# Windowed attention and a gated network on one Trainium2 core: weights by 1024 columns, values in one load, first keys copied, second unit's steps by twos

## The chip, the cores and the metric

The kernel runs on one core of a Trainium2 chip. The metric is the device time of one execution in microseconds (us), lower being better. The core has five engines that take their instructions in order and wait for each other by semaphores: TensorE (PE in the profile; PEld is its loading of weights), VectorE (DVE), ScalarE (ACT), GpSimd (POOL) and SyncE (SP), which here issues nearly all loads.

## The reference

```
attention: q, k, v are (4, 8, 768, 64)
k_sum = max of k over blocks of 32 rows;  v_sum = mean of v over blocks of 32 rows
scores_l = scale * q k^T, masked to |i - j| < 16
scores_s = scale * q k_sum^T + log(32)
a = softmax of the two side by side;  out = a @ [v; v_sum]
network: x is (3072, 512), the attention's output by tokens
h = ((x @ w1) * (x @ w2)) @ w3          w1, w2: (512, 1024), w3: (1024, 1024)
return h @ w_out                        w_out: (1024, 512)
```

The network's weights are 64-bit floats; q, k, v are 32-bit.

## The kernel before

**Network.** `w3 @ w_out` is folded once into eight tiles `wp` (`fold_weights`, L192). Then, for each unit of 512 tokens (six units), `gate` (L413) makes eight hidden tiles `h` out of w1 and w2, and `project` (L445) multiplies them by `wp`. Every product is split in a high and a low part and costs three matmuls with 512 columns (`products`, L110): 192 matmuls for the fold, and 192 for the gates and 96 for the projections of one unit.

**Weights.** A weight arrives as pairs of 32-bit words. `weight` and `start_loads` (L127, L135) load it in pieces of 512 columns (512 KB) into a ring of ten tiles, on SP. `convert` (L151) makes floats of it: a Prelu on ScalarE for every piece (L166), on VectorE a shift (L174) and for every piece a shift-and-or (L177), then the high part by a cast on ScalarE (L187) and the low part by a subtraction on VectorE (L108, in the helper `low`). Most weights have 1024 columns in two pieces; wo 0 and w3 0 to 3 are handled by halves.

**Attention.** A step is one unit with one of four pairs of heads, 24 steps. `load_scores` (L297) loads q and k, k in four windows of 160 columns with a gap of 24 into which `gather` (L305) copies the block summaries on GpSimd; `load_values` (L277) loads the values in three DMAs and `load_sums` (L286) adds the value means. Then: scores on TensorE (L320), masking and maximum on VectorE (L334), exponential on ScalarE (L348), reciprocal (L353, L354), normalization, transposes on TensorE (L374), copies `pt` out of PSUM (L379 to L383), outputs on TensorE (L394) and x (L405, L108). The summaries of batch 0 come from whole keys (`load_keys`, L222; `summaries`, L227) and from value rows whose block means TensorE makes (`mean_products`, L256); those of batch 1 are loaded as eight `raw` tiles through two buffers (`load_second`, `second_batch`).

**Order.** The first two units (steps 0 to 7) run in a loop whose counter `t` counts weight pieces. `LOADS` (L598) tells which input is loaded after which piece, `WORK` (L614) what else is done at which `t`, `FIRST` at which `t` a step begins: its scores are issued there, and at the next step's `t` its transposes and copies, its outputs one `t` later. After this, `run` (L499) issues so many columns of the network's products to TensorE, as far as their weights are there: `RATE` a step of the loop, `LATER_RATE`, and at last an even share of what is left up to the end of the first unit. In this loop SP and TensorE keep the program's order; the other engines' order is made by the planner. After it, the steps 8 to 23 run by twos in slots, with two steps' scores beside the transposes and outputs of the two before, and a stretch of the network behind them. `NORMALIZE` tells for each of the steps 0 to 7 whether ScalarE (A, eight instructions, L363) or VectorE (V, one, L365) normalizes, `SECOND` who makes the second copy `pt`.

Of the kernel before, what the change touches and what calls it, by code (L numbers as in the profile page):

```python
# [11 lines left out]
F32 = mybir.dt.float32  # L12
# [15 lines left out]
PIECE = 512  # L28
AHEAD = 4

FIRST = (15, 18, 20, 22, 27, 32, 37, 44)
# [3 lines left out]
EARLY = (  # L35
    *(("wo", 0, 0), ("w3", 0, 0), ("wo", 0, 1), ("w3", 1, 0), ("wo", 1), ("w3", 2, 0), ("w3", 3, 0)),
    *(("w3", 0, 1), ("w3", 1, 1), ("wo", 2), ("w3", 2, 1), ("w3", 3, 1), ("wo", 3)),
)
# [9 lines left out]
NORMALIZE = "VAAAAAAA"  # L48
SECOND = "AAAVAVVA"
SOONER = 400  # L50
RING = 10
# [19 lines left out]
def attention_moe(ctx, tc, qG, kW, kT, vP, vW, vB, mask, w1, w2, w3T, wo, out):  # L71
    nc = tc.nc
    B, NPAIR, _, S = kT.shape
    NB = S // BLOCK
# [20 lines left out]
    ident = const.tile([P, P], F32, name="ident")  # L95
    make_identity(nc, ident)
    mask_sb = const.tile([P, 3, KR], F32, name="mask_sb")

    mean_sb = const.tile([P, S // P * NB], F32, name="mean_sb")
    nc.gpsimd.memset(mean_sb, 0.0)  # L100
    for i in range(P // BLOCK):
        part = mean_sb[i * BLOCK : (i + 1) * BLOCK, i : S // P * NB : NB + P // BLOCK]
        nc.gpsimd.memset(part, 1.0 / BLOCK)
# [23 lines left out]
    def weight(name, i, src, shape, part=None):  # L127

        n = src.shape[1] // 2
        parts = range(n // PIECE) if part is None else [part]  # L130
        units.append((name, i, shape, list(parts), len(todo) + len(parts) - 1))
        for k in parts:
            todo.append(src[:, 2 * k * PIECE : 2 * (k + 1) * PIECE])

    def start_loads(at_least):  # L135

        while todo or due_loads:
            if len(loading) >= at_least and len(loading) + len(working) + len(kraws) + len(vraws) + made[0] + 2 >= RING:
                return
# [8 lines left out]
            due_loads.extend(LOADS.pop(begun[0], ()))  # L148
            begun[0] += 1

    def convert(name, i, shape, parts, last):  # L151


        n = len(parts) * PIECE
        f = sb.tile([P, 2 * PIECE], F32, name="wf", bufs=5)[:, :n]
        bits = f.bitcast(U32)
        low_words = []
# [3 lines left out]
        for k in range(len(parts)):  # L161
            raw = loading.pop(0)
            working.append(raw)
            words = raw.rearrange("p (n t) -> p n t", t=2)
            low_words.append(words[:, :, 0])
            nc.scalar.activation(  # L166
                f[:, k * PIECE : (k + 1) * PIECE],
# [51 lines left out]
    def held(b):  # L219
        return {"bufs": 2} if b else {"tag": "ring", "bufs": RING}  # L220

# [555 lines left out]
```

## Time and profile before

| | |
|---|---|
| timed runs | 538.26, 538.26, 539.84 us (median 538.26) |
| profiled execution | 540.01 us, span 537.9 us |
| busy share of the span | PE 96%, PEld 78%, ACT 45%, DVE 44%, POOL 11% |
| granted TensorE clock, mean | 0.994 |
| moved by DMA | 67.21 MB |

The span goes from the first to the last instruction. A line such as L320 is a line of the program below. In the lists, a group gives line, engine, operation, written and read tiles and their shapes, the count, the busy time in us, the mean of one in ns, and then the idle time of the engine before it and what ended it ("<-"). In the chain of waits each row is start, length and what the end of the program waited for at that time.

### The profile page before, as it was taken

To read this page: it belongs to the slowest core of one execution; us is meant where nothing else is said; L and a number is where in the kernel's file an instruction comes from. 1 tells how busy PE (TensorE), PEld (TensorE's weight loads), DVE (VectorE), ACT (ScalarE), POOL (GpSimd) and SP (SyncE) were. 2 spreads that over 40 slices of the span, in tenths; PEclk is the share of its full clock that TensorE was granted. 3 is DMA by queue.
4 is the path that set the end of the run, shared out by engine and by line. 5 is a ranking of instruction groups with operands and counts; after the bars stand their busy time and mean duration, and the time that the engine had idled before them with its cause. 6 is when DMAs were issued, how large, how long until landed. Compare 5 with 4: busy or idle time off the path is not lost.

```text
span 537.9 us, 9987 instructions
## 1 busy us (share of the span) xinstructions
PE 514.2 (96%) x3888; PEld 419.8 (78%) x3888; DVE 237.2 (44%) x686; ACT 239.7 (45%) x691; POOL 56.8 (11%) x99
## 2 busy tenths in 40 slices
PE   2877999999999999999999999999999999999997
PEld 1655777778778888888888888888888888888885
DVE  4878989998404236634244033251042250122210
ACT  5548998886436226226245144262162361222210
POOL 0020121111002101103003003011011030000000
PEclk9988999999999999999999999999999999999999
DMA  8999899595524005544041141050160021000001
GB/s 300 399 347 346 219 293 372 172 295 172 177 76 153 0 1 169 160 125 142 0 125 45 40 151 60 0 165 25 40 190 1 1 75 39 22 19 0 1 19 58
DMA packets 30574, 67.21 MB, mean 125 GB/s; under 512 B 4032, under 2 KB 7616, under 8 KB 30528
## 3 DMA queue, kind: packets, MB, share of 16 engines
q1 hardware_dynamic: 27072, 60.30, 35.5%
q10 hardware_dynamic: 3456, 6.29, 3.2%
q8 instruction: 30, 0.49, 0.4%
q14 instruction: 16, 0.13, 0.1%
HBM read 58.51 MB, written 6.29 MB: 120 GB/s over the span
## 4 chain that ended last, share of the span: by engine, by line
PE 83%; DMA 9%; ACT 5%; DVE 1%; issue 0%; SPq 0%; ACTq 0%
PE mm L112 74%; DMA wraw<-in_w3T_dram 5%; PE po L394 4%; PE sc L320 3%; DMA raw<-in_kT_dram 3%; PE tp L374 2%; DMA v<-in_vW_dram 2%; ACT sm L348 2%; ACT sm L363 1%; ACT w L187 1%; ACT wf L166 1%; ACT pt L379 0%; DVE wf L177 0%; ACT x L405 0%; ACT wp L210 0%
## 5 line engine op out<-in xcount | busy, mean ns | idle before, releaser
L112 PE MATMUL mm<-x,w 128*128 128x512 f32 x1152 | 265.2, 390 | 0.0
L112 PEld LDWEIGHTS mm<-x,w 128*128 128x128 f32 x1152 | 215.3, 188 | 46.0 <-DVE w L108 0.3
L112 PE MATMUL mm<-wp,h 128*128 128x512 f32 x576 | 134.0, 391 | 0.0
L112 PEld LDWEIGHTS mm<-wp,h 128*128 128x128 f32 x576 | 107.5, 188 | 22.8 <-issue 0.2
L348 ACT ACTIVATE sm<-sm,mx 128x120 f32<-128x120 f32 x192 | 73.6, 388 | 19.9 <-DVE mx L334 19.9
L439 DVE TENSOR_TENSOR g<-mm,g 128x512 f32<-128x512 f32 x48 | 33.1, 689 | 89.3 <-PE mm L112 87.5
L440 ACT CAST h<-g 128x512 fp32r<-128x512 f32 x48 | 29.7, 618 | 88.4 <-DVE g L439 88.4
L112 PE MATMUL mm<-w,w 128*128 128x512 f32 x192 | 53.0, 428 | 12.6 <-ACT w L187 11.4
L112 PEld LDWEIGHTS mm<-w,w 128*128 128x128 f32 x192 | 37.3, 202 | 25.0 <-ACT w L187 13.3
L458 ACT COPY o<-mm 128x512 f32<-128x512 f32 x24 | 14.0, 585 | 81.4 <-PE mm L112 81.4
L108 DVE TENSOR_TENSOR h<-g,h 128x512 fp32r<-128x512 f32 x48 | 35.9, 748 | 25.1 <-ACT h L440 24.8
L436 ACT COPY g<-mm 128x512 f32<-128x512 f32 x48 | 28.0, 583 | 34.5 <-PE mm L112 34.1
L334 DVE CUSTOM_DVE_ANT_0 sm<-sc,mask_sb 128x120 f32<-128x120 f32 x192 | 40.9, 275 | 2.9 <-PE sc L320 2.9
L383 DVE COPY pt<-tp 120x512 f32<-120x512 f32 x19 | 12.4, 687 | 67.6 <-PE tp L374 67.6
L307 POOL COPY k<-ks 128x96 f32<-128x96 f32 (+1 forms) x32 | 9.8, 316 | 257.3 <-DMA k<-in_kW_dram 194.7
L348 ACT ACTIVATION_READ_ACCUMULATOR sm<-sm,mx 128x1 f32 x192 | 36.7, 191 | 0.0
L108 DVE TENSOR_TENSOR x<-po,x 128x512 fp32r<-128x512 f32 x24 | 16.6, 691 | 42.3 <-ACT x L405 42.3
L166 ACT ACTIVATE wf<-wraw 128x512 f32<-128x512 f32 x40 | 26.4, 673 | 8.3 <-DMA wraw<-in_wo_dram 3.9
L357 POOL TENSOR_TENSOR sm<-sm,mx 128x960 f32<-128x960 f32 x16 | 29.1, 1820 | 6.0 <-DVE mx L354 5.0
L394 PEld LDWEIGHTS po<-pt,v 120*64 120x64 f32 x768 | 23.9, 138 | 5.8 <-issue 2.5
L108 DVE TENSOR_TENSOR w<-wf,w 128x1024 fp32r<-128x1024 f32 (+1 forms) x25 | 25.4, 1015 | 5.8 <-ACT w L187 5.5
L394 PE MATMUL po<-pt,v 120*64 120x64 f32 x768 | 26.3, 224 | 1.6 <-ACT pt L379 1.4
(33 smaller groups left out, 273.2 us busy)
## 6 DMA issues: line engine op xcount, KB each, us to landing
k<-in_kW_dram SPq DMA_DIRECT2D x24, 368.0 KB
wraw<-in_w3T_dram SPq DMA_DIRECT2D x16, 512.0 KB
wraw<-in_w_dram SPq DMA_DIRECT2D x16, 512.0 KB
q<-in_qG_dram SPq DMA_DIRECT2D x24, 256.0 KB
raw<-in_kT_dram SPq DMA_DIRECT2D x16, 384.0 KB
out_dram<-o ACTq DMA_DIRECT2D x24, 256.0 KB
v<-in_vW_dram SPq DMA_DIRECT2D x24, 192.0 KB
raw<-in_vB_dram SPq DMA_DIRECT2D x12, 384.0 KB
```

Source lines behind the costliest of these rows:

```text
L108: eng.tensor_tensor(dst, src, hi.bitcast(F32), ALU.subtract)
L112: nc.tensor.matmul(acc, lhsT=a, rhs=b, start=first and i == 0, stop=last and i == len(terms) - 1)
L166: nc.scalar.activation(f[:, k * PIECE : (k + 1) * PIECE], words[:, :, 1].bitcast(F32), AF.Prelu, scale=2.0**-112, alpha=-(2.0**32),)
L320: nc.tensor.matmul(sc[h][64 * g : 64 * g + 64, i * KR : (i + 1) * KR], lhsT=q[rows, i * P + 64 * g : i * P + 64 * g + 64], rhs=k[rows, i, ...
L334: nc.vector.tensor_tensor_reduce(out=sm[:, j], in0=sc[h][:, i * KR : (i + 1) * KR], in1=mask_sb[:, 0 if blk == 0 else 2 if blk == BLOCKS - ...
L348: nc.scalar.activation(sm[:, j], sm[:, j], AF.Exp, bias=mx[:, 0, j : j + 1], scale=-1.0, accum_out=mx[:, 1, j : j + 1])
L357: nc.gpsimd.tensor_tensor(sm, sm, mx[:, 2].unsqueeze(2).broadcast_to([P, NI, KR]), ALU.mult)
L394: nc.tensor.matmul(po[cols, at : at + 64], lhsT=v[:, g, i, cols], rhs=pt[g][:, (h * NBLK + i) * 64 : (h * NBLK + i + 1) * 64], start=True, ...
L436: nc.scalar.copy(g, a[:, :U])
L439: nc.vector.tensor_tensor(g, acc[1][:, :U], g, ALU.mult)
L440: nc.scalar.copy(h[:, 0], g)
L458: nc.scalar.copy(o, acc[:, :DO])
```

## The change

- `PIECE` is 1024 and the ring has five tiles of double size, with two loads ahead instead of four. A weight of 1024 columns is one load of 1 MB, and its Prelu, shift, shift-and-or, cast and subtraction are one instruction each. Only the first two weights are still converted by halves of 512. w3's first four tiles are stored so that one load holds half of two of them (`w3h`).
- Hidden tiles `h` lie in pairs in one ring tile. Whole keys and value rows of batch 0 take the buffers of x (six) instead of the ring's.
- A step's values come in one DMA, with zero rows where the means are added.
- The first unit's steps no longer load k: `windows` copies it on GpSimd out of the whole keys, in two copies a step.
- `FIRST` is now (12, 18, 20, 23, 46, 62): steps 0 to 3 begin one by one at the first four, and step 3's transposes wait for 46. Steps 4 and 5 begin together at 46; at 62 their transposes and outputs are issued and steps 6 and 7 begin. The transposes and outputs of 6 and 7 move into the first slot. Before the slots, the network is issued up to 0.96 of the first unit instead of all of it.
- `NORMALIZE`, `SECOND`, `LOADS`, `WORK` and the rates have new values; P stands for GpSimd. Steps 0 and 1 transpose into the scores' PSUM banks. The copies out of the folded products have a higher priority.

```diff
-PIECE = 512
-AHEAD = 4
-FIRST = (15, 18, 20, 22, 27, 32, 37, 44)
+PIECE = 1024
+AHEAD = 2
+FIRST = (12, 18, 20, 23, 46, 62)
-EARLY = (
-    *(("wo", 0, 0), ("w3", 0, 0), ("wo", 0, 1), ("w3", 1, 0), ("wo", 1), ("w3", 2, 0), ("w3", 3, 0)),
-    *(("w3", 0, 1), ("w3", 1, 1), ("wo", 2), ("w3", 2, 1), ("w3", 3, 1), ("wo", 3)),
-)
+EARLY = (("wo", 0), ("w3h", 0), ("wo", 1), ("w3h", 2), ("w3h", 1), ("wo", 2), ("w3h", 3), ("wo", 3))
-NORMALIZE = "VAAAAAAA"
-SECOND = "AAAVAVVA"
+NORMALIZE = "APAPPVVV"
+SECOND = "VVAVVAVV"
+BANKS = "SSTTTTST"
-RING = 10
+RING = 5
...
-            if len(loading) >= at_least and len(loading) + len(working) + len(kraws) + len(vraws) + made[0] + 2 >= RING:
+            if len(loading) >= at_least and len(loading) + len(working) + (made[0] + 1) // 2 + 1 >= RING:
...
+        n = PIECE // 2 if first < 4 else PIECE
+        parts = [slice(k, k + n) for k in range(0, PIECE, n)]
...
-        return {"bufs": 2} if b else {"tag": "ring", "bufs": RING}
+        return {"bufs": 2} if b else {"tag": "x", "bufs": 6}
...
-        nc.sync.dma_start(v[:CUT, 0], vW[u, p, 0])
-        nc.sync.dma_start(v[: CUT - 64, 1], vW[u, p, 1, : CUT - 64])
-        nc.sync.dma_start(v[KR - 64 :, 1], vW[u, p, 1, CUT - 64 :])
+        nc.sync.dma_start(v, vW[u, p])
...
-        nc.sync.dma_start(k, kW[p, :, u * NBLK : (u + 1) * NBLK])
+        if u:
+            nc.sync.dma_start(k, kW[p, :, u * NBLK : (u + 1) * NBLK])
         return q, k
+
+    def windows(k, raw):
+
+        for to, at in ((k[:, :, :CUT], 0), (k[:, :, CUT + NB :], CUT)):
+            nc.gpsimd.tensor_copy(to, raw[:, at : at + U].rearrange("p (i c) -> p i c", c=P)[:, :, : to.shape[2]])
...
+        if NORMALIZE[s] != "A":
+            eng = nc.vector if NORMALIZE[s] == "V" else nc.gpsimd
+            eng.tensor_tensor(sm, sm, mx[:, 2].unsqueeze(2).broadcast_to([P, NI, KR]), ALU.mult)
...
-        h = sb.tile([P, 2, U], F32R, name="h", tag="ring", bufs=RING)
+        if f % 2 == 0:
+            pair_of_h[0] = sb.tile([P, 2, 2, U], F32R, name="h", tag="ring", bufs=RING)
+        h = pair_of_h[0][:, f % 2]
...
+    TO_SLOTS = ALL_FOLD + 0.96 * UNIT
...
+    def two_pairs(s):
+
+        both = [begin(p) for p in (s, s + 1)]
+        yield
+        for p, (u, sm, mx, sc) in zip((s, s + 1), both):
+            reduce(u, 0, sc, sm, mx)
+            reduce(u, 1, sc, sm, mx)
+            expose(0, sm, mx)
+            yield
+            expose(1, sm, mx)
+            invert(mx)
+            yield
+            normalize_alone(p, sm, mx)
+
+    def four_pairs(s):
+
+        steps = two_pairs(s)
+        yield from steps
+        while t[0] < FIRST[-1]:
+            yield
+        steps = two_pairs(s + 2)
+        tps = [transposes(sms.pop(p)[0], **more) for p, more in zip((s, s + 1), ({}, SPARE))]
+        pts = [evacuate(tp, SECOND[p]) for p, tp in zip((s, s + 1), tps)]
+        next(steps)
+        for p, pt in zip((s, s + 1), pts):
+            keep_x(outputs(pt, values.pop(p)), xs[place(p)[0]])
+        yield
+        yield from steps
...
+    def first_keys(p):
+        raw = kraws.pop(p)
+        windows(inputs[p][1], raw)
+        summaries(0, p, raw)
...
     LOADS = {
+        4: [lambda: keys(0)],
         7: [lambda: nc.sync.dma_start(mask_sb, mask)],
+        8: [lambda: fetch(0)],
+        9: [lambda: rows(1)],
+        11: [lambda: fetch(1)],
+        15: [lambda: rows(2), lambda: rows(0)],
+        16: [lambda: keys(1), lambda: keys(2)],
+        17: [lambda: fetch_values(0), lambda: keys(3)],
+        18: [lambda: fetch(2)],
+        23: [lambda: fetch_values(1), lambda: fetch_values(2)],
+        25: [lambda: fetch(3)],
+        26: [lambda: fetch_values(3)],
     }
     WORK = {
+        11: [lambda: first_keys(0), lambda: fill(0)],
+        13: [means],
+        17: [lambda: load_second(2), lambda: fetch_sums(0)],
+        18: [lambda: first_keys(1), lambda: fill(1)],
+        20: [lambda: first_keys(2), lambda: fill(2)],
+        21: [lambda: load_second(0), lambda: load_second(1), lambda: fetch(5), lambda: fetch_sums(2)],
+        22: [lambda: second_batch(0), lambda: load_second(3), lambda: load_second(4), lambda: first_keys(3), lambda: fetch(4), lambda: fill(3), lambda: fetch_sums(1)],
+        23: [lambda: second_batch(1)],
+        24: [lambda: load_second(5)],
+        25: [lambda: second_batch(2), lambda: second_batch(4), lambda: load_second(6)],
...
+        31: [lambda: second_batch(5)],
...
+        34: [lambda: fill(4)],
...
+        40: [lambda: fill(5)],
...
     }
-    RATE = 6600
-    LATER_RATE = 6944
+    RATE = 8000
+    LATER_RATE = 2744
...
-                due = given[0] + (ALL_FOLD + UNIT - given[0]) / max(1, FIRST[-1] + 7 - t[0])
-            run(min(due, ALL_FOLD + UNIT))
+                due = given[0] + (TO_SLOTS - given[0]) / max(1, FIRST[-1] + 5 - t[0])
+            run(min(due, TO_SLOTS))
...
-            last = (s - 2, s - 1) if s > NFIRST else ()
+            last = (s - 2, s - 1)
```

216 lines of the change are left out of this document (104 added, 112 removed).

## The prediction

> **What bounds the kernel now.** I read the page's head first, then the chain of waits, then TensorE's timeline in the first 90 us, and last the groups and windows of that stretch.
>
> ```profile
> span 537.9 us, 9987 instructions
> PE 514.2 (96%) x3888; PEld 419.8 (78%) x3888; DVE 237.2 (44%) x686; ACT 239.7 (45%) x691; POOL 56.8 (11%) x99
> ```
>
> The profiled execution took 540.01 us, 2.1 us more than its span; the three timed runs have a median of 538.26 us. I work out a difference against the profiled execution and take it off the median. A difference of 0.3% (1.6 us) is about what a measurement of this kernel can tell from none.
>
> TensorE is busy 96% of the span, so only its waits can be won. The chain of waits (start, length, what) says where they lie:
>
> ```profile
> 86.19 0.04 issue
> 86.24 1.15 PE po L394 x32
> 87.39 13.84 PE mm L112 x60
> 101.23 0.61 PE tp L374 x16
> 101.84 0.98 PE sc L320 x32
> 102.83 3.67 PE mm L112 x15
> 106.49 1.08 PE po L394 x32
> ...
> 278.57 32.86 PE mm L112 x144
> ...
> 534.42 0.59 ACT o L458
> ```
>
> From 86.24 us on the chain is TensorE's almost without a break. So the end is (the moment at which the gates of the first unit begin, 87.4 us) + (TensorE's work from there on). I call that moment G. A change that doesn't alter the products moves the end one for one with G, plus any wait that it makes later. Prices of TensorE's pieces: 0.228 us a product (32.86/144), 0.61 for a step's transposes, 0.98 for its scores, 1.08 for its outputs.
>
> Before G, TensorE's own timeline and windows of the stretch show what was lost:
>
> ```profile
> 36.03 0.64 PE L261 MATMUL means<-rows,mean_sb 128*24 128x128 f32 x16 [2.63 <-DMA rows<-in_vP_dram]
> 49.82 0.69 PE L374 MATMUL tp<-ident,sm 64*120 64x64 f32 x16 [3.37 <-DVE sm L365]
> 86.24 1.15 PE L394 MATMUL po<-pt,v 120*64 120x64 f32 x32 [1.21 <-ACT pt L379]
> ```
>
> ```profile
> 0.00:87.00 87.00, 66.98 (x586) 49.81 (x588) 69.31 (x161) 63.23 (x160) 12.31 (x32) 0.96 0.97 323
> 10.00:30.00 20.00, 16.93 (x57) 11.22 (x57) 17.20 (x28) 11.90 (x19) 0.00 (x0) 1.00 1.03 400
> 36.00:40.00 4.00, 3.97 (x38) 2.79 (x42) 1.91 (x3) 2.65 (x6) 2.76 (x4) 0.62 1.04 356
> 50.00:54.00 4.00, 4.00 (x52) 3.28 (x50) 3.93 (x7) 2.69 (x4) 0.00 (x0) 0.57 1.02 332
> 60.00:80.00 20.00, 19.83 (x219) 15.44 (x219) 17.34 (x55) 20.00 (x70) 3.93 (x9) 1.00 0.86 246
> ```
>
> (Columns of the second: stretch, then busy us of PE, weight loads, DVE, ACT, POOL, then granted clock, DMA share, GB/s.) The products for the block means end at 36.67. Between them and G stand, in program order, 126 of the 192 weight-folding products, four steps' transposes, five steps' scores and four steps' outputs: 126 x 0.228 + 4 x 0.61 + 5 x 0.98 + 4 x 1.08 = 40.4 us. 36.67 + 40.4 = 77.1, and G was 87.4. So 10.3 us were lost after the means: 3.4 waiting for step 0's normalization, 1.2 for step 3's copy, 1.5 and 1.7 to a clock of 0.62 and 0.57 in the 4 us after an idle stretch, the rest in small pieces while ScalarE was busy 20.00 of 20 us.
>
> **The change part by part.**
>
> *The means.* They wait for the three loads of value rows. Ahead of the last of those in SP's order before: 16 weight pieces, mask, one q, one k, two sets of whole keys. After: 8 weight pieces of double size, mask, two q, one set of keys.
>
> ```profile
> k<-in_kW_dram SPq DMA_DIRECT2D x24, 368.0 KB
> q<-in_qG_dram SPq DMA_DIRECT2D x24, 256.0 KB
> raw<-in_kT_dram SPq DMA_DIRECT2D x16, 384.0 KB
> ```
>
> That is 368 + 384 - 256 = 496 KB less, less 8 KB for the padding: 1.2 us at the 400 GB/s of 10 to 30 us. Means end at 35.4. The first product now needs 2 MB instead of 1 MB, 2.6 us later at that rate; the idle time before the means hides it, and without that cover it costs 2.6.
>
> *TensorE's order after the means.* By the step at which each weight is ready, 20 products (60 matmuls) stand before the means instead of 66 matmuls, so 132 follow. Step 3's transposes and outputs, and the gates, are moved from loop step 27/28 to 46/47; between the end of the fold (25) and 46 nothing else is issued to TensorE, so its order keeps its form, with one exception: the scores of step 5 now stand ahead of step 3's outputs and of the gates, not only those of step 4. Work: 132 x 0.228 + 4 x 0.61 + 5 x 0.98 (scores 1 to 5) + 4 x 1.08 = 41.8 us. Floor of G: 35.4 + 41.8 = 77.2. The 0.98 of step 5 comes off the work behind G.
>
> *ScalarE and VectorE until G.* The groups:
>
> ```profile
> L166 ACT ACTIVATE wf<-wraw 128x512 f32<-128x512 f32 x40 | 26.4, 673 | 8.3 <-DMA wraw<-in_wo_dram 3.9 <-DMA wraw<-in_w3T_dram 2.3 <-DMA wraw<-in_w_dram 2.0
> L187 ACT CAST w<-wf 128x1024 fp32r<-128x1024 f32 x15 | 15.7, 1049 | 6.2 <-DVE wf L177 6.1
> L177 DVE SCALAR_TENSOR_TENSOR wf<-wraw,wf 128x512 uint32<-128x512 uint32 x40 | 26.3, 685 | 0.5
> L108 DVE TENSOR_TENSOR w<-wf,w 128x1024 fp32r<-128x1024 f32 x15 | 18.5, 1233 | 4.2 <-ACT w L187 4.2
> L363 ACT ACTIVATE sm<-sm,mx 128x120 f32<-128x120 f32 x56 | 17.9, 395 | 0.9 <-DVE mx L354 0.9
> L383 DVE COPY pt<-tp 120x512 f32<-120x512 f32 x3 | 2.1, 687 | 1.1 <-PE tp L374 1.1
> L365 DVE TENSOR_TENSOR sm<-sm,mx 128x960 f32<-128x960 f32 x1 | 1.2, 1151 | 0.0
> L357 POOL TENSOR_TENSOR sm<-sm,mx 128x960 f32<-128x960 f32 x2 | 4.0, 2018 | 0.3 <-DVE mx L354 0.3
> ```
>
> A 1024-wide Prelu doesn't occur: between 1.05 (the 1024-wide cast) and 1.35 us (two of 512); I take 1.10, since the cast does the same pass. 14 units are converted up to G, 12 of them now in one piece: 12 x (1.35 - 1.10) = 3.0 us off ScalarE. The 1024-wide L177: between 1.23 (L108 of that width) and 1.37; I take 1.23, because it too reads two SBUF operands: 12 x 0.14 = 1.7 us off VectorE. Normalization of steps 0 to 3 was V, A, A, A and is A, P, A, P: ScalarE does 16 passes of 0.395 instead of 24 (-3.2), VectorE loses 1.15, GpSimd gains two of 2.02. Second copies were A, A, A, V and are V, V, A, V: two of about 0.6 leave ScalarE, 2 x 0.69 come to VectorE. Sums until G: ScalarE 7.4 us less, VectorE -1.7 - 1.2 + 1.4 = 1.5 less. From the 0:87 row, VectorE needs some 68 of its 69.3 us; its first work can begin at about 6 us, so its floor for G is 74, below TensorE's 77.2. ScalarE's is near 62. So the next bound is TensorE itself.
>
> *Step 0 is begun earlier.* Its whole keys are the first input loaded and it begins at loop step 12 instead of 15, with more products between its scores and its transposes. The 3.4 us wait and the slow clock behind it (1.7) go. The slow clock after the means (1.5) stays. The Trainium skill ("TensorE: Matmul & The Clock Gate", the HAM clock gate) says that an idle window of about 3.4 us halves the clock until one has been busy; the two rows fit, and by that rule a shorter gap before the means would save that 1.5 too. I keep it.
>
> *Moved copies.* The first unit's k loads (4 x 368 KB, 3.8 us of DMA time) become two GpSimd copies a step. On GpSimd's queue stand behind them the filling-in of the summaries, the inversions and the value sums. Nearest rows:
>
> ```profile
> 32.20 0.58 POOL L307 COPY k<-ks 128x96 f32<-128x96 f32 x1 [30.33 <-DVE ks L229]
> 40.68 0.26 POOL L307 COPY k<-ks 128x96 f32<-128x96 f32 x1
> 75.61 0.22 POOL L307 COPY k<-ks 128x48 f32<-128x48 f32 x1
> ```
>
> (0.26 - 0.22)/48 is 0.8 ns an element, so 384 and 256 elements take about 0.5 and 0.4 us: 0.9 a step alone, twice that beside VectorE's work. Steps 0, 2 and 3 have their keys long before; step 1's lie under the products of the fold. Nothing on the path; 0.9 to 1.8 if step 1's keys come late.
>
> *One load of values a step* issues one DMA instead of three, and moves 480 KB instead of 384 (zero rows): 0.25 us a step, off the path. *Halved ring of doubled tiles, hidden layer in pairs*: same bytes, nothing.
>
> *New waits.* Step 1's normalization on GpSimd takes 2.0 instead of eight passes; I allow 1 us before its transposes. Step 5's scores need the second batch's keys for it, loaded late on SP's queue (worked out with the first rival); I allow 1.5. With the clock (1.5), 4.0 us are lost after the means instead of 10.3. G = 77.2 + 4.0 = 81.2, 6.2 earlier.
>
> *Behind G.* The second unit's steps go by twos: 4 and 5 right before G, 6 and 7 at loop step 62, with two transposes moved into the first slot of the main loop. Between the scores of 6 and 7 and their transposes lie two outputs and some 33,700 columns (66 products), 17 us; the chain of two steps on VectorE and ScalarE needs 13 to 15. I allow 1.0 us for a wait there (0 to 3). The later slots are unchanged.
>
> Sum: -6.2 (G) - 1.0 (scores of 5 already done) + 1.0 = -6.2. The profiled 540.01 becomes 533.8, the median 538.26 becomes 532.0.
>
> **The rivals.**
>
> *Slower: the scores of step 5 hold the gates.* In SP's order the keys for step 5 stand behind q 4, which waits for the scores of step 3 to free a buffer, behind values 3 and behind two-buffer loads of the second batch. All of TensorE waits in order behind scores 5. The waits exist already:
>
> ```profile
> SPq L281 <- PE po L394: 20.8, 4, 12.6
> SPq L301 <- PE sc L320: 9.1, 4, 3.6
> SPq L239 <- DVE ks L229: 8.1, 3, 6.2
> ```
>
> Behind scores 3, SP has still to load q 4 and k 4 (624 KB), a weight (1024), values 3 (480) and then these keys (384): 2.5 MB, 6.3 us at 400 GB/s, and a summary on VectorE and a copy on GpSimd follow. TensorE needs from scores 3 to scores 5 another 30 matmuls, one step's outputs, one's transposes and one's scores: 6.8 + 1.1 + 0.6 + 1.0 = 9.5 us. So the two are about level, which is why I allow 1.5. If one more wait of the 12.6 us kind stands ahead, G is 81.2 + 11 = 92 and the end 543. It decides from 6 us of extra delay on. Against: values 3 wait only for outputs 1, which come well before.
>
> *No change: GpSimd and VectorE hold each other up.* The copy of 96 elements took 0.58 us while VectorE was busy and 0.26 while it wasn't. GpSimd's new work until G is 4 x 0.9 + 2 x 2.02 = 7.6 us. If VectorE stands still for all of it, its floor is 74 + 7.6, and with half of the 12 us that it idled besides (81.4 - 69.3), G is 87.6 and the end 538.4. The Trainium skill ("SBUF — State Buffer", on the shared port pair) says that a GpSimd instruction and a VectorE instruction with two SBUF inputs lock each other out for a whole instruction; by that rule this case is full. The rows show GpSimd held up, not VectorE.
>
> *Bigger gain: no new wait.* If neither step 1 nor step 5 waits and the clock stays up, G is 77.2, or 75 with the means at 33; no wait at 62: end 526 to 528.
>
> **How the numbers follow.** The forecast (529 to 535.5) gets 0.48, the bigger gain 0.15, no or little change 0.17 (half of it between 535.5 and 536.6), slower 0.20. So faster by over 0.3%: 0.71; within: 0.09; slower: 0.20. The range leaves out the far end of the bigger gain and of the slower case: 526 to 542.
>
> **What would show it.** Right: the first matmuls of the gates near 81 us; no wait of TensorE for the normalization of step 0; ScalarE below 18 of 20 us between 60 and 80; the chain TensorE's from G on; the scores of 4 and 5 back to back ahead of outputs 3. Wrong: a gap of over 3 us ahead of scores 5 or outputs 3; GpSimd copies of over 1 us with idle VectorE beside them; TensorE waiting at the first slot; means later than 37.

## The result and the profile after

| | before | changed |
|---|---|---|
| median of 15 runs each, in turn | 539.02 us (537.99 to 542.32) | 536.72 us (533.69 to 538.96) |
| profiled execution | 540.01 us, span 537.9 | 535.38 us, span 533.6 |

The ratio is 0.9949, with a 95% interval of 0.9929 to 0.9968: faster by 2.3 us in the medians where 6.2 were forecast. The measured time lies within the range, and the sign and the place were right. The two profiled executions differ by 4.63 us, twice as much as the medians: that of before lay 0.99 above the median of its 15 runs, that of the changed kernel 1.34 below its own (4.63 = 2.30 + 0.99 + 1.34). The profiled execution of the changed kernel was a lucky one: it is one of the five of its fifteen runs with a mean granted clock of 0.999 or 1.0, and these have a mean of 534.9 us, the other ten, at 0.987 to 0.997, one of 537.3.

The head of the changed kernel's page:

```profile
span 533.6 us, 9786 instructions
PE 508.3 (95%) x3888; PEld 418.7 (78%) x3888; DVE 239.2 (45%) x667; ACT 224.8 (42%) x627; POOL 71.4 (13%) x110
```

TensorE's timeline up to the gates (start, length, what, and in brackets how long it stood idle before and what ended that):

```profile
30.89 1.51 PE L268 MATMUL means<-rows,mean_sb 128*24 128x128 f32 x48
32.88 0.51 PE L113 MATMUL mm<-w,w 128*128 128x512 f32 x1 [0.48 <-ACT w L190]
34.76 8.22 PE L113 MATMUL mm<-w,w 128*128 128x512 f32 x35 [1.37 <-DVE w L109]
42.91 0.68 PE L391 MATMUL tp<-ident,sm 64*120 64x64 f32 x16
...
44.51 4.38 PE L113 MATMUL mm<-w,w 128*128 128x512 f32 x18
48.82 1.15 PE L411 MATMUL po<-pt,v 120*64 120x64 f32 x32
49.90 1.66 PE L113 MATMUL mm<-w,w 128*128 128x512 f32 x6
51.49 1.05 PE L334 MATMUL sc<-k,q 64*64 64x120 f32 x32
...
59.52 0.34 PE L411 MATMUL po<-pt,v 120*64 120x64 f32 x4 [0.45 <-issue]
60.34 1.03 PE L411 MATMUL po<-pt,v 120*64 120x64 f32 x28 [0.49 <-POOL v L303]
...
66.83 1.05 PE L334 MATMUL sc<-k,q 64*64 64x120 f32 x32
...
78.31 0.69 PE L391 MATMUL tp<-ident,sm 64*120 64x64 f32 x16 [2.07 <-POOL sm L380]
78.92 1.46 PE L334 MATMUL sc<-k,q 64*64 64x120 f32 x48
82.01 0.64 PE L334 MATMUL sc<-k,q 64*64 64x120 f32 x16 [1.63 <-POOL k L321]
82.58 1.15 PE L411 MATMUL po<-pt,v 120*64 120x64 f32 x32
83.67 16.62 PE L113 MATMUL mm<-x,w 128*128 128x512 f32 x72
```

The gates begin at 83.67 (G), 3.7 us sooner than before's 87.4. The means end at 32.40, 4.3 sooner than in the execution of before that the prediction read (in a second one, below, they end at 35.51 and wait for nothing, so 3.1 sooner than there). Step 0's transposes (42.91) wait for nothing any more. Two new waits stand right ahead of the gates: step 3's transposes wait 2.07 for their normalization on GpSimd, and the second half of step 5's scores waits 1.63 for summaries in its keys. VectorE stands behind both. The maxima of step 3, whose scores end at 67.88, are taken from 70.89 on, after work that VectorE does without a break. The summary for step 5 (L236) follows the conversion of a weight, which had waited for its Prelu on ScalarE:

```profile
77.96 0.84 DVE L173 TENSOR_SCALAR wf<-wf 128x1024 uint32<-128x1024 uint32 x1 [1.54 <-ACT wf L164]
79.32 1.42 DVE L176 SCALAR_TENSOR_TENSOR wf<-wraw,wf 128x1024 uint32<-128x1024 uint32 x1
80.67 0.94 DVE L236 TENSOR_REDUCE ks<-raw 128x24 f32<-128x768 f32 x1
```

Whether the keys themselves had landed long before 80.67 the trace doesn't show.

The windows (busy us of PE, weight loads, DVE, ACT, POOL; granted clock, DMA share, GB/s):

```profile
0.00:87.00 87.00, 67.42 (x639) 51.97 (x640) 71.93 (x147) 59.84 (x136) 24.38 (x41) 1.00 0.94 321
60.00:80.00 20.00, 17.30 (x213) 13.84 (x217) 16.90 (x39) 13.75 (x36) 9.18 (x12) 1.00 0.85 256
```

ScalarE is relieved as the prediction said (13.75 of 20 us, before 20.00), and the clock of this execution is 1.00 throughout. VectorE is not relieved: up to G it is busy 69.53 us, before 69.70 (up to 87.39).

### The profile page after: what moved, and what is told of

The parts are those of the page before. It is cut to its first block, busy times and chain, and to the rows that moved or that the text cites. A ratio compares the mean times of both kernels' runs of the same rounds, so it can differ in the third digit from the quotient of the medians.

```text
span 533.6 us, 9786 instructions
## 1 busy us (share of the span) xinstructions
PE 508.3 (95%) x3888; PEld 418.7 (78%) x3888; DVE 239.2 (45%) x667; ACT 224.8 (42%) x627; POOL 71.4 (13%) x110
## 4 chain that ended last, share of the span: by engine, by line
PE 76%; DMA 12%; DVE 6%; ACT 3%; issue 1%; SPq 1%; POOL 0%; DVEq 0%; ACTq 0%; POOLq 0%
PE mm L113 66%; DMA wraw<-in_w_dram 4%; PE po L411 4%; PE sc L334 4%; DMA raw<-in_vB_dram 3%; DMA rows<-in_vP_dram 2%; PE tp L391 2%; DMA v<-in_vW_dram 2%; DVE wf L176 2%; DVE w L109 1%; ACT wf L164 1%; DMA wraw<-in_wo_dram 1%; DVE wf L173 1%; DVE ks L236 1%; DVE wp L109 1%
## 5 line engine op out<-in xcount | busy, mean ns | idle before, releaser
L456 DVE TENSOR_TENSOR g<-mm,g 128x512 f32<-128x512 f32 x48 | 33.1, 689 | 87.7 <-PE mm L113 86.8
L113 PE MATMUL mm<-w,w 128*128 128x512 f32 x192 | 49.9, 412 | 14.6 <-ACT w L190 11.9
L109 DVE TENSOR_TENSOR h<-g,h 128x512 fp32r<-128x512 f32 x48 | 35.4, 741 | 26.1 <-ACT h L457 25.9
L400 DVE COPY pt<-tp 120x512 f32<-120x512 f32 x22 | 14.3, 684 | 67.4 <-PE tp L391 67.4
L321 POOL COPY k<-ks 128x96 f32<-128x96 f32 (+1 forms) x32 | 11.9, 380 | 234.8 <-DMA k<-in_kW_dram 217.2
L190 ACT CAST w<-wf 128x1024 fp32r<-128x1024 f32 (+1 forms) x22 | 21.3, 967 | 18.5 <-DVE wf L176 18.4
L109 DVE TENSOR_TENSOR x<-po,x 128x512 fp32r<-128x512 f32 x24 | 16.6, 690 | 26.9 <-ACT x L422 26.8
L164 ACT ACTIVATE wf<-wraw 128x1024 f32<-128x1024 f32 (+1 forms) x22 | 23.0, 1057 | 13.2 <-DMA wraw<-in_w_dram 8.4
L109 DVE TENSOR_TENSOR w<-wf,w 128x1024 fp32r<-128x1024 f32 (+1 forms) x22 | 24.9, 1135 | 4.8 <-ACT w L190 4.8
```

The lines of the kernel that those rows point to most:

```text
L109: eng.tensor_tensor(dst, src, hi.bitcast(F32), ALU.subtract)
L113: nc.tensor.matmul(acc, lhsT=a, rhs=b, start=first and i == 0, stop=last and i == len(terms) - 1)
L164: nc.scalar.activation(f[:, some], words[:, some, 1].bitcast(F32), AF.Prelu, scale=2.0**-112, alpha=-(2.0**32),)
L190: nc.scalar.copy(t[:, 0, some], f[:, some])
L456: nc.vector.tensor_tensor(g, acc[1][:, :U], g, ALU.mult)
```

## The experiments

Two things had to be explained: what the gain is made of, and why it is smaller than forecast. In the expectations, A is the theory that the moment G decides, which TensorE's waits ahead of it set: early begin of step 0, then the two new waits; A1 says that these waits cover each other (take one away and the next shows), A2 that they add up. B says that the work taken off ScalarE is what counts. C says that the slow granted clock after idle gaps makes the rest. The ratios are all to the kernel before, run on the same chip; the changed kernel stands at 0.9949.

**The kernel before once more.** Nothing is edited.

> The kernel before, unchanged, timed once more with the granted clock of each run. Theory C (the size of the gain was misjudged because the two profiled runs caught different clocks): its runs spread with their clock, those at 0.999 or 1.0 below 537.5 us and those at 0.99 or less near 540, as the fifteen runs of the changed kernel do (534.9 against 537.3 on the mean). Rival: the clock is the same in all runs (0.994) and the spread of 538 to 542 has another cause; then the clock has no part in the misjudged size.

Ratio 0.9991 (0.9974 to 1.0008). Its profiled execution took 538.53 us, with G at 85.86: in the same kernel G lies 1.5 us apart in two executions, and the end with it. Its ten runs (537.65 to 541.45 us) don't spread with their clock (0.990 to 0.994): the one at 0.990 took 538.34, one at 0.993 took 541.45. So for the kernel before the rival of theory C holds; the changed kernel's runs do spread with theirs.

**Undoing parts of the change.** Engines as before:

```diff
-NORMALIZE = "APAPPVVV"
-SECOND = "VVAVVAVV"
+NORMALIZE = "VAAAAAAA"
+SECOND = "AAAVAVVA"
```

> The changed kernel with the old engines for normalization and second copies (ScalarE for nearly all). Theory A (the moment G at which the first unit's gates begin is set by TensorE's order and by short waits in it): ScalarE has some 7 us more work up to G but idled there; G moves by at most 2 us from 83.7, either way, since step 3's normalization leaves GpSimd. Theory B (ScalarE was the bound, its relief is the gain): G goes back to about 87 and the time to that of the kernel before, within 0.2%.

Ratio 0.9995 (0.9971 to 1.0020), G 86.93: about the whole gain is gone. Theory B alone isn't shown by that: the waits moved too, step 3's transposes now waiting 1.73 us for ScalarE, and G is later by the clock as well (0.84 at 33 to 44 us, where the 35 products after the means took 9.85 us instead of 8.22, and 0.56 at 82 to 88).

Step 0 begun late: `FIRST[0]` is 15 instead of 12.

> The changed kernel with step 0 begun at loop step 15 as before, instead of 12. Theory A: a wait for step 0's normalization ahead of its transposes comes back, 2 to 4 us, with a slow clock behind it; G at 86 to 89, the time 0.4 to 0.8% above the changed kernel's. Rival: the fold's products behind the means hide step 0's chain in either place; G stays at 83.7 within 1 us.

Ratio 1.0062 (1.0042 to 1.0082), 6 us over the changed kernel. Step 0's old wait is back, and larger:

```profile
47.82 2.36 PE L391 MATMUL tp<-ident,sm 64*120 64x64 f32 x16 [5.78 <-ACT sm L377]
```

This is theory A's first half, with a longer wait than the 2 to 4 us that it named; the second half of step 5's scores waits longer too, 3.23 us. Undoing the early begin costs more than the whole gain.

Keys of the first unit loaded again instead of copied (`if u:` becomes `if True:`, the call of `windows` left out).

> The first unit's keys are loaded again (four loads of 368 KB) instead of being copied by GpSimd out of the whole keys; nothing else changes. If the copies were free and the loads aren't (3.7 us of DMA time, most of it ahead of the second-batch loads), the loads behind scores 3 come up to 1 us later: means 0.5 to 2 us later, gates at 84.5 to 86, ratio 0.996 to 0.999. If the copies hold VectorE up beside them (the rival, the port), gates come 0.5 to 1.5 us sooner, 82 to 83, ratio 0.992 to 0.994.

Ratio 1.0080 (1.0048 to 1.0113), far over what either theory said (its profiled execution, 546.76 us, is the slowest of six). On GpSimd's timeline the order has changed. Here first the kernel with the loads, then the changed kernel:

```profile
59.61 1.38 POOL L303 COPY v<-vs 24x512 f32<-24x512 f32 x1 [2.42 <-DMA v<-in_vW_dram]
61.08 2.11 POOL L380 TENSOR_TENSOR sm<-sm,mx 128x960 f32<-128x960 f32 x1
```

```profile
54.58 1.79 POOL L380 TENSOR_TENSOR sm<-sm,mx 128x960 f32<-128x960 f32 x1 [0.70 <-DVE mx L368]
56.44 3.82 POOL L303 COPY v<-vs 24x512 f32<-24x512 f32 x4
```

The planner put a copy of value sums, which waits for its load, ahead of step 1's normalization (L380). GpSimd takes its work in order, so the normalization, whose maxima were ready at 57.8, began at 61.08, and TensorE waited 4.96 us for it. The run doesn't give the price of the four loads; it shows what one place in a queue can cost.

Conversions by halves of 512 everywhere (`n = PIECE // 2`).

> All weights are loaded by 1024 columns but converted by halves of 512, not only the first four pieces. By the prices of the groups ScalarE does 0.2 us more for each conversion and each copy and VectorE 0.14 to 0.2 for each of its three operations: up to the gates some 10 pieces, so 4 us more on ScalarE and 4 to 5 on VectorE. If VectorE sets the moment of the gates (busy 71.9 of 87 us), gates at 86 to 88, ratio 0.999 to 1.002. If loads and single waits set it (the theory), gates at 84 to 85.5, ratio 0.996 to 0.999.

Ratio 1.0091 (1.0061 to 1.0121); G 92.02. Missed by both theories again, and for the same kind of reason. VectorE in that kernel:

```profile
62.92 0.20 DVE L368 RECIPROCAL mx<-mx 128x8 f32<-128x8 f32 x1 [1.48 <-POOL mx L367]
63.92 0.68 DVE L400 COPY pt<-tp 120x512 f32<-120x512 f32 x1
```

Step 1's transposes were done at 57.7, but the copy of their result (L400) stands behind the next step's reciprocal, which waits for GpSimd, busy with value sums until 62.6. Step 1's outputs begin 5.56 us late. VectorE isn't alone in this: ScalarE's copy of the other half stands behind a Prelu that waits for its weight until 63.09, and ends at 64.74, VectorE's at 64.60. Either would have held the outputs.

Values in three loads instead of one (480 KB back to 384):

```diff
-        nc.sync.dma_start(v, vW[u, p])
+        nc.sync.dma_start(v[:CUT, 0], vW[u, p, :CUT, 0])
+        nc.sync.dma_start(v[: CUT - 64, 1], vW[u, p, : CUT - 64, 1])
+        nc.sync.dma_start(v[KR - 64 :, 1], vW[u, p, KR - 64 :, 1])
```

> A step's values come in three loads instead of one (384 KB instead of 480), nothing else. I had costed the one load at nothing. If that is right, the gates stay at 83 to 84.5 us and the ratio at 0.993 to 0.997. If the bytes saved count (0.25 us a step, four steps ahead of the gates), 0.5 to 1 us sooner: ratio 0.992 to 0.994. If SP's issuing of two more transfers a step counts (0.33 to 0.45 us each), or the planner's order changes, gates later than 85 and ratio 0.997 or above.

Ratio 0.9984 (0.9966 to 1.0003), G 87.25, with longer waits for step 3's normalization (3.07) and step 5's keys (2.23). The planner's orders changed here too, GpSimd's among them, and in this execution the 35 products after the means took 9.85 us at a reduced clock, so of the 1.9 us it isn't shown how much is SP's issuing. The parts undone one by one give 2.5, 6.1, 7.1, 7.7 and 1.9 us, in a change that gains 2.7 by these ratios: they are not terms of a sum.

**The waits ahead of the gates.** Step 3 normalized on VectorE (`NORMALIZE = "APAVPVVV"`):

> The changed kernel with step 3 normalized on VectorE instead of GpSimd; no other instruction moves. Theory A1 (two waits stand one behind the other: step 3's transposes wait 2.1 us for GpSimd, but behind them the second half of step 5's scores can't begin before 82.0 us, when its keys are there): the transposes come 1 us earlier, the wait of step 5's scores grows by the same 1 us, G stays at 83.7 within 0.4 us and the time at that of the changed kernel within 0.1%. Theory A2 (the GpSimd normalization was the mistake): G falls by 1 us or more, the time by 0.2 to 0.4%.

Ratio 0.9950 (0.9927 to 0.9973): nothing gained. The wait that was shortened came back further on:

```profile
78.21 0.68 PE L391 MATMUL tp<-ident,sm 64*120 64x64 f32 x16 [1.51 <-DVE sm L380]
...
83.30 0.64 PE L334 MATMUL sc<-k,q 64*64 64x120 f32 x16 [3.01 <-POOL k L321]
```

G is 84.95 in this execution: step 5's second half begins 1.3 later than at 82.01, where A1 had it stand still, because its summary is later (81.95), again behind the weight's conversion. That one wait takes over from the other is as A1 says; but the repetitions of the unedited kernel below have that second half at 82.95 to 83.64 too, so one execution doesn't prove it. The wait for the normalization is still 1.51 with VectorE in GpSimd's place, so GpSimd's slower multiplication isn't what makes most of it. Next, the keys of step 5 loaded first of the late loads (`load_second(5)` from `WORK` 24 to 22, ahead of `fetch(4)`):

> The changed kernel with the second batch's keys for step 5 loaded ahead of q and k of step 4, which wait for the scores of step 3; before, they stood behind them, a weight and values 3. Theory A1: the wait of step 5's scores (1.6 us) goes, and VectorE's summary and copy in front of step 3's outputs move ahead too; the wait of step 3's transposes for GpSimd stays. G falls by 1 to 2 us, to 81.7 to 82.7. Theory A2: G falls by less than 0.5 us. Theory C (slow clock after the gaps near 80 us in most timed runs): the mean clock rises and the median falls by more than G does in the profile.

Ratio 0.9982 (0.9962 to 1.0002). Step 5's scores don't wait; values 3 are late in their place. SP's queue shows why, and TensorE's timeline what it did:

```profile
66.33 3.92 SPq L231 DMA_DIRECT2D raw<-in_kT_dram  x2
70.34 0.38 SPq L309 DMA_DIRECT2D q<-in_qG_dram  x1
```

```profile
83.45 0.34 PE L411 MATMUL po<-pt,v 120*64 120x64 f32 x4 [2.49 <-POOL v L303]
```

The last of three `raw` loads in a row (one at 64.52 and these two) waits for one of the second batch's two buffers, and on SP's queue q 4, k 4, a weight and values 3 stand behind that wait; q 4 is issued at 70.34 instead of 67.96. With step 3's normalization on VectorE besides:

> Both edits at once. Theory A1: neither wait covers the other any more; G falls by 2.5 to 3.5 us against the changed kernel, to 80.2 to 81.2, which is what the prediction had; time 0.5 to 0.6% below the changed kernel's, 1.0 to 1.1% below the kernel's before. Theory A2: the gain is that of the normalization alone, 1 us. Theory C adds: clock at 0.997 or above in most runs.

Ratio 1.0001 (0.9989 to 1.0014), outputs 3 waiting 3.37 us. And with values 2 moved behind as well (`fetch_values(2)` and its sums from 23 and 21 to 22):

> Both edits and the values of step 2 loaded later, so that SP does not stand 13 us (from 37 to 50 us) waiting for step 0's outputs to free their buffer with the next weight, q 3 and the second batch behind it. Theory A1 with SP's stand as a third cause: these loads start 6 us or more earlier, but nothing on TensorE waits for them once the keys of step 5 are moved: G at 80 to 81 as with the two edits, within 0.7 us. Rival (the stand of SP is what keeps the weights and so G late): G falls by another 2 us or more, below 79.

Ratio 1.0037 (1.0020 to 1.0055). Now step 2 pays:

```profile
75.59 0.48 PE L411 MATMUL po<-pt,v 120*64 120x64 f32 x4 [5.08 <-POOL v L303]
```

Three misses of one kind: SP's queue carries all these loads in one bundle, and whatever is put ahead pushes something that is needed as soon. What can give way is a load that is not: the weight w2_0, which the gates read only 2.7 us after G.

```diff
-        26: [lambda: fetch_values(3)],
...
-        ... lambda: fetch(4), lambda: fill(3), lambda: fetch_sums(1)],
+        ... lambda: fetch(4), lambda: load_second(5), lambda: fetch_values(3), lambda: fill(3), lambda: fetch_sums(1)],
...
-        24: [lambda: load_second(5)],
```

> Keys of step 5 and values 3 both move ahead of the weight w2_0 on SP's queue (one megabyte, 2.5 us at 400 GB/s); nothing else changes. If what is left of the waits ahead of the gates is one bundle of loads behind scores 3 (the theory), both come 1.5 to 2.5 us sooner: scores 5 wait 0 to 0.3 us instead of 1.63, outputs 3 don't wait, only the 2.07 us for step 3's normalization stays. Gates at 81.7 to 82.3 us instead of 83.67, and the median 1 to 2 us under the changed kernel's (ratio 0.991 to 0.993). If the buffers set these loads and not the bytes ahead of them (the rival), they land where they did, gates stay at 83.4 to 84 and the ratio at 0.995. If w2_0 becomes the next late load, the gates begin at 82 but wait over 1 us within their first 3 us, ratio 0.995 or above.

Ratio 0.9931 (0.9905 to 0.9957). The waits ahead of the gates went as the theory had it, and a smaller one came up behind them:

```profile
79.14 0.69 PE L391 MATMUL tp<-ident,sm 64*120 64x64 f32 x16 [1.85 <-POOL sm L380]
79.76 3.18 PE L334 MATMUL sc<-k,q 64*64 64x120 f32 x64
...
84.24 2.33 PE L113 MATMUL mm<-x,w 128*128 128x512 f32 x9
87.21 0.73 PE L113 MATMUL mm<-x,w 128*128 128x512 f32 x2 [0.64 <-ACT x L422]
```

All 64 matmuls of the scores of 4 and 5 stand together. G was expected at 81.7 to 82.3 and is 84.24: the stretch up to step 3 came 0.8 us later in this execution, since the 35 products after the means took 9.86 us instead of 8.22, and the scores took 3.18 us at a reduced clock instead of some 2.0. The new wait, 0.64 and then 0.22 us, is for step 3's x: ScalarE's cast of it (at 86.59, in the changed kernel at 83.78) now stands behind the cast of a weight that waits 2.02 us for VectorE. Nor did only the loads move: VectorE makes step 5's summary at 77.17 instead of 80.67, ahead of the next weight's conversion, so how much is due to SP's queue and how much to VectorE's isn't told apart. With step 3 on VectorE too:

> As the kernel with the weight behind, and step 3's normalization on VectorE instead of GpSimd. Theory (chained waits): with the keys of step 5 and values 3 sooner, the wait ahead of step 3's transposes falls from 2.07 to 0.5 to 1.5 and nothing takes its place: gates at 80.8 to 81.5, ratio 0.989 to 0.991. Rival (each wait moved uncovers the next, whatever load it is): gates at 82 or later and ratio 0.993 or above.

Ratio 0.9932 (0.9908 to 0.9956), median 535.37 us beside 538.95 for before, G 82.87; the wait for step 3's normalization is 2.29, not shorter, and that for x is 0.84 and 0.21. The intervals of these two overlap with the changed kernel's, so that they beat it is likely and not shown.

**The clock.** Forty useless products at the start and eight ahead of the means:

> The changed kernel with 40 extra products of the identity with itself on TensorE ahead of the first real one and 8 ahead of the means, so that it does not stand idle there; they write a PSUM tile that nothing reads. Theory C: the clocks of the timed runs come together near 1.0, the spread shrinks, and the median falls from 536.7 towards 535, although the program has more work. Rival: clocks and median stay as they are within 0.2% (or the 8 products ahead of the means delay the rest by up to 2 us): the slow stretches lie elsewhere.

Ratio 1.0069 (1.0052 to 1.0086). The first forty held TensorE until 13.6 us and the planner reordered ScalarE and VectorE; the run answers nothing about the clock. Then useless products only inside the waits, four ahead of step 3's transposes and three within the scores of step 5:

> The changed kernel with useless products of the identity on TensorE where it waited ahead of the gates: four ahead of step 3's transposes (wait of 2.07 us), three in the middle of the scores of step 5 (1.63 us). Nothing else is added; a product of 128 columns took 0.11 to 0.28 us for each of its two passes, so they fit within the waits. Theory (the idle gaps let the granted clock fall in most runs and that is the part of the 4.6 us of the profiled execution that the medians don't show): clock 0.996 or above in nearly all runs, median 534.5 to 535.5 on this measure, ratio 0.991 to 0.993, and the gates still at 83.5 to 84.3 us. Rival (the clock falls in some runs whatever TensorE does there, or in another place): clock again 0.987 to 1.0, ratio 0.994 to 0.997.

Ratio 0.9995 (0.9970 to 1.0019): a miss. The clock rose a little, but the planner's orders changed from there on, and the second half of step 5's scores now waits 3.28 us. The same in the kernel with the weight behind:

> The kernel with the weight w2_0 behind the keys of step 5 and values 3, with four useless products ahead of step 3's transposes, the one wait of over 1.5 us that it has there. Theory: no gap is left between 70 and 84 us, clock 0.996 or above in nearly all runs, median 1 to 2 us under that of the kernel without the products (ratio 0.989 to 0.991). Rival: ratio 0.993 to 0.995 with clocks of 0.994 to 0.997 as there.

Ratio 1.0011 (0.9986 to 1.0037), with a wait of 1.28 for ScalarE's copy for outputs 3 that it didn't have, and 1.57 for x, where it had 0.64 and 0.22. That filling the gaps would help is not shown. What shows where the time goes is plainer: the changed kernel, not edited, under the profiler three more times.

> The changed kernel, unchanged, once more under the profiler: what does an ordinary execution look like beside the profiled one of 535.38 us at a clock of 1.00? If the clock makes the difference (theory), an execution of 537 us or more shows a stretch of granted clock under 0.9 at 30 to 42 or 76 to 90 us, and the same waits within 0.3 us. If waits make it (rival), its clock is near 1.00 and the waits for step 3's normalization, step 5's keys, values 3 or behind the gates are longer by what is missing.

> As the first repetition: theory, slow executions show low clock in rows of 30 to 42 or 76 to 90 us with the same waits; rival, longer waits at full clock.

> As the first repetition: theory, slow executions show low clock in rows of 30 to 42 or 76 to 90 us with the same waits; rival, longer waits at full clock.

They took 537.37, 539.34 and 537.51 us. The window from 76 to 94 us, first in the execution of 535.38, then in the three (the third last number is the granted clock):

```profile
76.00:94.00 18.00, 14.30 (x159) 11.77 (x158) 13.07 (x17) 9.12 (x11) 7.16 (x8) 1.00 1.03 316
```

```profile
76.00:94.00 18.00, 14.13 (x141) 11.74 (x142) 10.83 (x15) 7.56 (x9) 6.63 (x7) 0.72 1.02 304
```

```profile
76.00:94.00 18.00, 13.70 (x150) 11.52 (x151) 11.40 (x15) 8.48 (x11) 6.03 (x6) 0.91 1.04 286
```

```profile
76.00:94.00 18.00, 14.78 (x154) 12.19 (x153) 11.96 (x16) 8.36 (x10) 6.33 (x7) 0.91 1.02 288
```

And TensorE's timeline in the first repetition:

```profile
78.12 0.68 PE L391 MATMUL tp<-ident,sm 64*120 64x64 f32 x16 [2.19 <-POOL sm L380]
78.73 2.47 PE L334 MATMUL sc<-k,q 64*64 64x120 f32 x48
82.95 1.08 PE L334 MATMUL sc<-k,q 64*64 64x120 f32 x16 [1.76 <-POOL k L321]
83.96 1.97 PE L411 MATMUL po<-pt,v 120*64 120x64 f32 x32
```

The waits are the same within 0.13 us; the same 48 matmuls take 2.47 us instead of 1.46, the outputs 1.97 instead of 1.15. G is 85.86, 85.29 and 85.09 in the three, beside 83.67. In the first repetition the whole difference lies here: G is 2.19 later, the span 2.0 longer. In the second and third the wait for step 5's keys differs too (2.15 and 1.15); there the 48 matmuls take 2.68 and 2.59 us, and the transposes of the third 1.11 instead of 0.69. In the second a further part comes behind G (its span is 3.9 longer, its G 1.6 later). So an ordinary execution of the changed kernel has its gates near 85 us, and up to G it is the reduced clock around the two new gaps that takes most of the difference. That the gaps bring the clock down fits these traces, but no run shows it: `fill` and `w2_fill` didn't take the waits away. The Trainium skill ("TensorE: Matmul & The Clock Gate", Part 1) says that the clock gate looks at windows that run freely and don't start with the kernel; by that rule the same gap falls differently on the windows from one execution to the next. Four executions of one kernel with gaps alike within a microsecond and clocks of 1.00, 0.72, 0.91 and 0.91 are in keeping with it and don't prove it. The idle window of about 3.4 us that the prediction drew on doesn't fit so well: no gap at 76 to 94 us in these four was longer than 2.31 us, and the prediction's own two slow rows followed gaps of 2.63 and 3.37. In the second execution of before, which has no wait at the means, the clock at 36 to 40 us is 1.00; at 50 to 54, behind a wait of 3.54, it is 0.67.

## Why the prediction was right in sign and wrong in size

**G sets the end: right.** The span less G is 450.5 us in both profiled executions of before, and 449.9, 449.7, 452.2 and 450.6 in the four of the changed kernel. The 1.0 that I allowed for a wait at the slots and the 1.0 taken off for the scores of 5 cancel in the sum, but not for the reason given: the transposes that I feared for (134.50) wait for nothing, while TensorE waits 0.68 us at 109.13 for g (L456) and 1.31 at 216.34 for h (L109), where before has one wait of 0.20 behind G. By the starts, the work by twos pays for them, which I hadn't priced: up to the next unit's gates TensorE has three runs of products where before has nine, and a run costs some 0.22 us (below).

**The basis of the sum: wrong.** "I work out a difference against the profiled execution and take it off the median" holds only if both profiled executions stand at the same place among their runs. They stood 0.99 above and 1.34 below their medians. What was missing is a term for the clock in an ordinary run: I kept 1.5 us of slow clock after the means, where this execution has none; the three repetitions lose it at 76 to 94 us, behind gaps that I had priced as waits alone. The 1.5 itself was a fair size: of the fourteen executions here that share the stretch up to step 0's transposes, five take 9.8 us for the 35 products after the means instead of 8.2.

**The means: right in direction, too small.** 1.2 us sooner by bytes was forecast, 4.3 came. The bytes weren't what mattered. SP's issue of the last of the three row loads, before and after:

```profile
25.54 0.38 SPq L253 DMA_DIRECT2D rows<-in_vP_dram  x1
```

```profile
16.18 1.25 SPq L260 DMA_DIRECT2D rows<-in_vP_dram  x2
```

It goes out 8 us sooner. Before, its issue had waited 1.1 us for a weight's conversion on VectorE (L177), the rows drawing on the ring of the weights, which they no longer do; what each part of the change gives here no run tells apart. TensorE waits for nothing at the means; its own order bounds them at 30.89.

**The allowance of 4.0 us between the means and G: wrong; it was 9.5** (83.67 - 32.40 - 41.8, with the prediction's 41.8 us of work). That is the step that failed: waits and work that it put at nothing. Its terms:
- The wait for step 0's normalization went, as forecast, and `undo_early` shows that it comes back. No slow clock there in this execution: 1.5 less than allowed.
- The loss "in small pieces" of before (10.3 less the named 3.4, 1.2, 1.5 and 1.7: 2.5 us) I counted as gone with ScalarE's relief. It stayed: 9.5 less all waits shown above and one of 0.29 at step 2's transposes leaves 2.7 us. They aren't waits but work, for which my prices were too low. The 0.228 of a product came from a run of 144; between other work a run of 6 takes 1.59 us from its start to the next (49.90 to 51.49) and one of 18 takes 4.31 (44.51 to 48.82), which is 0.228 a product and some 0.22 for the run. By their starts the 132 products take 32.2 us instead of 30.1; the other 0.6 is in transposes, scores and outputs. Before has nine such runs after its means too, by that price 2.0 of its 2.5.
- With the means sooner, the products behind them wait for weights: 0.48 + 1.37 = 1.85, not foreseen.
- Step 1's normalization on GpSimd, for which I allowed 1.0, costs nothing, but step 3's costs 2.07, by the chain through VectorE shown above more than by GpSimd (1.51, 2.03 and 2.29 in three of the four runs with VectorE in its place; in the fourth, step 2's wait of 5.08 comes first); and step 1's outputs wait 0.45 + 0.49 for GpSimd's value sums.
- Step 5's keys: allowed 1.5, measured 1.63. That the two are close is luck: from scores 3 to the second half of step 5's I had 9.5 us of TensorE's work, and 6.3 for the loads with a summary and a copy behind them. TensorE's work was 10.4, and step 5's second half began 14.1 us after scores 3 (67.88 to 82.01); of the 3.7 that TensorE stood idle in between, step 3's normalization had taken 2.07.

Together -1.5 + 2.7 + 1.85 + 0.29 + 1.07 + 0.94 + 0.13 = +5.5, which is 9.5 instead of 4.0; the earlier means give 3.0 of it back, and G is 83.67 instead of 81.2.

**Prices of the other engines' operations.** The groups of the changed kernel:

```profile
L164 ACT ACTIVATE wf<-wraw 128x1024 f32<-128x1024 f32 x18 | 20.5, 1144 | 9.6 <-DMA wraw<-in_w_dram 8.4 <-DMA wraw<-in_w3T_dram 1.2
L176 DVE SCALAR_TENSOR_TENSOR wf<-wraw,wf 128x1024 uint32<-128x1024 uint32 x18 | 22.4, 1245 | 0.2
L380 POOL TENSOR_TENSOR sm<-sm,mx 128x960 f32<-128x960 f32 x3 | 5.4, 1791 | 1.3 <-DVE mx L368 1.0 <-DVE vs L254 0.3
```

1.14, 1.25 and 1.79 us where I took 1.10, 1.23 and 2.02; the copies of 384 elements 0.8 on the mean where I had 0.5 alone and twice that beside VectorE. These were good enough. What failed with VectorE was its sum, 1.5 us less up to G forecast and 0.2 measured, and the use of its floor of 74 us as a sign that it doesn't bind: its queue binds in single places all the same, as the two waits ahead of the gates show.

**The rivals.** *Slower by step 5's keys*: its mechanism is there, at 1.63 us instead of 12, and what is queued ahead of it on SP was named rightly. *GpSimd and VectorE hold each other up*: seen (below), for single instructions; what it adds to the waits listed no run tells apart. *Bigger gain*: no execution had it.

## What to carry to other kernels

A floor of work plus a few named waits is too low a time. Price a piece of work from rows where it stands as it will stand (a product from a run of 144 is too cheap for runs of 6 and 18), and don't count a loss as gone before its cause is named. Each wait that is removed uncovers the next one in the same in-order queue, so look for work that can give way rather than a load to bring forward, and follow the chain through every engine's queue, not the loads' alone. Before a difference of half a per cent is read off two profiled executions, see where each lies among its runs, and look at the granted clock behind every gap of more than a microsecond. With planner-made orders, undoing one part also moves others: compare the engines' orders before the time is taken as that part's price.

## What was not expected of the hardware

Around gaps of 2.07 to 2.31 and of 1.15 to 2.15 us, with the transposes and 48 scores between them, the granted clock fell in three of four executions, to a mean of 0.72 over 18 us in one; behind two gaps of 0.5 and 1.4 us after the means it was 0.84 at 33 to 44 us in five executions of fourteen. A copy of 48 elements on GpSimd, alone 0.22 us, took 2.76:

```profile
67.04 2.76 POOL L321 COPY k<-ks 128x48 f32<-128x48 f32 x1 [4.36 <-DMA k<-in_kW_dram]
73.59 0.22 POOL L321 COPY k<-ks 128x48 f32<-128x48 f32 x1 [3.79 <-DMA k<-in_kW_dram]
```

```profile
67.29 1.21 DVE L109 TENSOR_TENSOR w<-wf,w 128x1024 fp32r<-128x1024 f32 x1
68.51 1.22 DVE L176 SCALAR_TENSOR_TENSOR wf<-wraw,wf 128x1024 uint32<-128x1024 uint32 x1
```

VectorE ran two instructions with two SBUF operands at full speed in that time, 1.21 + 1.22 us, and the copy ended with the second: 2.43 + 0.22 is 2.65. It goes the other way round too. In the kernel that loads the first keys, VectorE's 1.25 us instruction took 2.69 beside GpSimd's normalization (61.08 to 63.19), and ended 1.08 after it:

```profile
61.58 2.69 DVE L176 SCALAR_TENSOR_TENSOR wf<-wraw,wf 128x1024 uint32<-128x1024 uint32 x1
```

The Trainium skill ("SBUF — State Buffer", on the shared port pair) says that of a GpSimd instruction and a VectorE instruction with two SBUF inputs the one that starts first holds the pair for its whole length. The second trace agrees, and for VectorE, which the rows of before had not shown as held up. The first agrees in that the copy got nowhere beside the two instructions, but it doesn't show who was first: the copy's row starts at 67.04, 0.25 us ahead of VectorE's first.
